# Two row-number tables instead of one, and a different placing of the first experts' reads, loads and splits, in an attention, ReLU-squared and routed-experts kernel

## The chip, the cores and the metric

The kernel runs on one core of one Trainium2 chip. The metric is device time in microseconds (us) of one execution, given as a median over runs.

## The reference

Three stages follow one another, all in float32 by value.

```python
# 1. attention, batch 4, 8 heads, 576 positions, 64 wide: a path downsampled by 4
#    (144 x 144, its result repeated 4 times) plus a local path, |i - j| < 4
x = (out_up + out_local)              # -> 2304 tokens x 512
# 2. a dense layer pair with squared ReLU (weights 512 x 2048 and 2048 x 512, stored as float64)
h = np.maximum(x @ w_in, 0.0)
x = (h * h) @ w_out
# 3. one expert of eight for each token
e_idx = np.argmax(x @ w_gate, axis=1)
gate_w = probs[np.arange(N), e_idx]   # softmax of x @ w_gate
eom = 1.0 / (1.0 + np.exp(-(x @ w_output_gate)))
for e in range(8):
    mask = e_idx == e
    ye = np.maximum(x[mask] @ w1[e], 0.0) @ w2[e]     # 512 -> 1024 -> 512
    out[mask] = gate_w[mask, None] * eom[mask, e, None] * ye
```

## The kernel before

**Dense stage.** The 2304 tokens are cut into nine chunks of 256 (`NCH = 9`), the 2048 hidden columns into 16 pieces of 128 (`NF = 16`, `FH = 8`). One step of the main loop does `l1(c, f)` (12 matmuls, line 473) for a piece f of a chunk c, and `l2` (6 matmuls, line 498) for the piece two steps back (`LAG = 2`). Every operand is held as two float32r parts, high and low, so a product is three matmuls. Between `l1` and `l2` of a piece stands a chain over three engines: ScalarE takes the ReLU out of PSUM (line 477), VectorE squares it and so frees the PSUM buffer (line 478), ScalarE rounds it to the high part (line 481), GpSimd subtracts to get the low part (line 482). There are two buffers of `ph` and of `g`, three of `gs`.

**Routing.** When a chunk's result is complete, `finish_y` copies it to SBUF and `routing` runs in three steps, interleaved with the next chunk's loop. It computes the gate scores, picks the expert of each token, computes the token's place in its expert's list, and then GpSimd writes the row numbers of the chunk's two tiles into a DRAM table `order` with two indirect DMAs of 128 four-byte elements each (line 586). A table `ytab` gets the rows themselves, from the SyncE queue (line 592). `order` has 8 lists of 2304 places; it is cleared at the start (line 168).

**First tiles.** In the last chunk (c = 8), at step f = 10, `first_rows` reads the first 128 places of the lists of experts 0 and 1 (tile `of`, line 657), casts them to integers on VectorE (line 659), gathers those rows (tile `xe`, line 662), and `first_part(0)` brings them through TensorE into PSUM (line 678). At the same step `experts[0].first()` and at f = 12 `experts[1].first()` load and split the four pieces of each expert's first weight matrix: a load is 512 KB on the SyncE queue into one of three buffers (tag `stg`, line 625), a split is a ScalarE copy of the piece (line 638) and a VectorE subtraction (line 639) of 128x1024 elements, after which the buffer is free again. At f = 14 the loads of the second matrix of expert 0 are written (line 628).

**After the last chunk.** The last chunk's routing adds its rows to the first tiles by matmuls with a one-hot matrix (line 712), writes its row numbers, and runs `first_layer(0)` (line 688). Then the whole table is read into `og` (line 838), transposed by TensorE (line 842), cast to `gi`, and used for all further gathers (line 878). By an issue-after edge `first_layer(1)` stands behind that transpose on TensorE. The second MoE stage then goes through the experts with branches on the number of tiles that each has.

The order of the instructions on each engine is chosen at build time by the scheduler of the framework, which may put an instruction ahead of the place where it is written. Each engine then takes its own instructions strictly in that order.

Of the kernel before, what the change touches and what calls it, by code (L numbers as in the profile page):

```python
# [10 lines left out]
F32 = mybir.dt.float32  # L11
F32R = mybir.dt.float32r
BF16 = mybir.dt.bfloat16
I32 = mybir.dt.int32
U32 = mybir.dt.uint32
AF = mybir.ActivationFunctionType
ALU = mybir.AluOpType
AX = mybir.AxisListType
#: Read as float32, the top half of a float64 times this has float32's exponent, three bits too low.
# [6 lines left out]
def attn_moe_kernel(  # L26
# [14 lines left out]
    nc = tc.nc  # L41
# [52 lines left out]
    order = dp.tile([E * NT, 1], F32, name="order")  # L94
# [16 lines left out]
    class Carved:  # L111
        """Buffers within larger tiles (each with the place that is free in it), by tag."""
# [55 lines left out]
    nc.gpsimd.dma_start(out=order.rearrange("(p c) o -> p (c o)", p=P), in_=none)  # L168
# [5 lines left out]
    def attention(b, hp, ap, psa):  # L174
# [51 lines left out]
        # local scores  # L226
# [86 lines left out]
        # downsampled P V  # L313
# [16 lines left out]
        # local P V  # L330
# [20 lines left out]
    def chain(units):  # L351
        """Units on one set of buffers: each starts in the middle of the one before it."""
        gens = [attention(*u) for u in units]

        def go(i, n):
            for _ in range(n if i < len(gens) else 0):
                next(gens[i], None)
                yield

        yield from go(0, 4)  # L360
        for i in range(len(gens)):
            yield from go(i, 3)
            yield from go(i + 1, 3)
            yield from go(i, 2)
            yield from go(i + 1, 1)
            yield from go(i, 1)
            if len(gens) == 1:
                yield from gens[i]
            else:
                go_on = gens[i]  # L370
                next(go_on, None)
                yield

# [14 lines left out]
    def f64_split(raw, hi, lo):  # L388
        """hi + lo of 512 columns of float64 words: float32's 24 bits, in two float32r parts."""
# [19 lines left out]
    def convert():  # L409
        """Both matrices of the first MoE in turn, a piece of 512 columns at a time."""  # L410
# [36 lines left out]
    def split_x(c, part):  # L447
        """The part of a chunk of x that is of its first (0) or another (1) of x's batches."""
        if c not in xc:
            xc[c] = mp.tile([P, 2, KC, CH], F32R, tag="xc", name=f"xc{c}")  # L450
        t, done = xc[c], 0
        while done < CH:
            b, s = divmod(c * CH + done, S)
            ln = min(CH - done, S - s)
            if part == (done > 0):
                for hp in range(HP):
                    src = carry[:, hp, :] if (c, part) == (2, 0) else xT[b, hp][:, s:s + ln]
                    hi = t[:, 0, hp, done:done + ln]
                    nc.scalar.activation(out=hi, in_=src, func=AF.Copy)
                    nc.vector.tensor_sub(out=t[:, 1, hp, done:done + ln], in0=src,  # L460
                                         in1=hi.bitcast(F32))
            done += ln
# [54 lines left out]
    def routing(c):  # L517
        """Puts the rows of y and their gates in ytab, their numbers in their experts' lists."""
# [66 lines left out]
        for i in range(2):  # L585
            nc.gpsimd.indirect_dma_start(  # L586
                out=order[:], out_offset=bass.IndirectOffsetOnAxis(ap=di[:, i:i + 1], axis=0),
# [21 lines left out]
    class Weights:  # L609
        """An expert's weights: four pieces for each layer are loaded, then put in two parts."""  # L610
# [30 lines left out]
        def first(self):  # L641
            self.place(0)
            for i in range(4):
                self.load(i)
                self.split(i)

# [6 lines left out]
    def first_rows():  # L653
        """What the first tiles of experts 0 and 1 hold before the last rows of y come."""
        of = const.tile([P, 2], F32, name="of")
        for i in range(2):
            nc.gpsimd.dma_start(out=of[:, i:i + 1], in_=order[NT * i:NT * i + P, :])
        oi = const.tile([P, 2], I32, name="oif")
        nc.vector.tensor_copy(oi, of)
# [11 lines left out]
        firsts.update(xe=xe, iota=iota2, xs=xs, hr=hrs)  # L671
        firsts["px"] = [first_part(0)]

# [19 lines left out]
    def last_rows(yr, dest, after):  # L693
        """The first tiles of experts 0 and 1, to which the last rows of y are added."""
# [89 lines left out]
    LAG, SX = 2, 4  # L784
    for s in range(len(seq) + LAG):
# [12 lines left out]
        if s < len(seq):  # L798
# [13 lines left out]
            if c == NCH - 1 and f == NF // 2 + 2:  # L812
                assert not routes
                first_rows()
                experts[0].first()
            if c == NCH - 1 and f == NF // 2 + 4:
                experts[1].first()
            if c == NCH - 1 and f == NF - 2:
# [14 lines left out]
    for i in range(3):  # L833
        experts[2].load(i, stages[i])

# [1 line left out]
    og = cv.tile([P, DM], I32, tag="tmp", name="og", bufs=TMPB).bitcast(F32)[:E * NTL // 2, 0:2 * P]  # L837
    nc.gpsimd.dma_start(out=og.rearrange("t (h p) -> t h p", h=2),
                        in_=order.rearrange("(t h p) o -> t h (p o)", h=2, p=P))
# [45 lines left out]
    def split_rows(xg, xs, g, name):  # L885
        """A tile's rows, transposed and in two parts; its gates and numbers to g."""
# [13 lines left out]
    def layer2(w2v, name):  # L900
        """The second layer of the tile that hs and gp belong to."""
# [14 lines left out]
    def hand_over(g, name, hr=hr):  # L916
        """The tile of hr and g becomes that of hs and gp."""
# [117 lines left out]
```

## Time and profile before

| | |
|---|---|
| median of 3 runs | 936.34 us |
| lowest and highest run | 930.26 and 936.98 us |
| profiled execution | span 932.8 us (the page gives no other time for it) |
| TensorE busy over the span | 854.6 us, 92% |
| VectorE, ScalarE, GpSimd busy | 426.7, 412.3, 361.5 us |
| DMA | 90.77 MB, mean 97 GB/s |

The profiled execution lies inside the spread of the runs, 3.5 us below their median. The rows further down come from it. Times in them are microseconds from the start of its span. PE is TensorE's matmuls, PEld its weight loads, DVE is VectorE, ACT is ScalarE, POOL is GpSimd, SP is SyncE; a q behind a name is the engine's own sequencer, where DMAs are issued. An arrow in brackets gives the idle time of the engine just before the row and what ended it.

### The profile page before, as it was taken

The page shows a single profiled execution, that of the slowest core. Times are in us where ns is not written, and L with a number is a line of the kernel's source. Part 1 is how long each engine was busy: PE and PEld are TensorE (multiplying, and loading weights), DVE is VectorE, ACT ScalarE, POOL GpSimd, SP SyncE. Part 2 cuts the span into 40 slices and gives each one's busy share as a digit, 9 for nine tenths or more (in the row PEclk, how much of TensorE's full clock was granted, in tenths as well). Part 3 has the DMA queues.
Part 4 walks back from the last instruction along what each step waited for, and adds up shares of the span by engine and source line. Part 5 has one row for each costly group of instructions (what it writes and reads, how often), then busy time and mean ns, then how long its engine had stood idle before and what let it go on. Part 6 is the DMA issues. An engine that isn't in the chain of part 4 may idle for free. (4 is left out here: it accounts for less than half of the span.)

```text
span 932.8 us, 16539 instructions
## 1 busy us (share of the span) xinstructions
PE 854.6 (92%) x6287; PEld 735.6 (79%) x6287; DVE 426.7 (46%) x910; ACT 412.3 (44%) x875; POOL 361.5 (39%) x450
## 2 busy tenths in 40 slices
PE   6568888999999999999999999778999899999995
PEld 5457677889989889889999899666777678878783
DVE  6999988533544433333222213332536564233110
ACT  6656556534454444443333324352536464243221
POOL 4876777542544533443222232342223322121111
PEclk9578988999999999999999999969999999999998
DMA  9963554111232212213000001754745944131111
GB/s 230 220 166 90 139 165 138 46 41 37 64 66 53 66 31 58 40 45 114 2 24 1 24 1 48 159 114 117 268 140 205 346 141 170 46 126 36 48 34 34
DMA packets 97602, 90.77 MB, mean 97 GB/s; under 512 B 64481, under 2 KB 77295, under 8 KB 97488
## 3 DMA queue, kind: packets, MB, share of 16 engines
q1 hardware_dynamic: 92096, 74.57, 27.9%
q0 software_dynamic: 5392, 14.74, 5.2%
q8 instruction: 65, 1.06, 0.5%
q14 instruction: 49, 0.40, 0.1%
HBM read 79.69 MB, written 10.38 MB: 97 GB/s over the span
## 5 line engine op out<-in xcount | busy, mean ns | idle before, releaser
L473 PE MATMUL ph<-xc,win 128*128 128x256 f32 x1728 | 254.1, 293 | 15.8 <-DVE g L478 8.1
L473 PEld LDWEIGHTS ph<-xc,win 128*128 128x128 f32 x1728 | 234.6, 195 | 30.4 <-DVE g L478 8.7
L498 PE MATMUL y<-wout,gs 128*128 128x512 f32 x864 | 232.0, 401 | 4.9 <-POOL gs L482 2.9
L482 POOL TENSOR_TENSOR gs<-g,gs 128x256 fp32r<-128x256 f32 x144 | 110.0, 767 | 189.2 <-ACT gs L481 107.4
L498 PEld LDWEIGHTS y<-wout,gs 128*128 128x128 f32 x864 | 152.7, 190 | 32.7 <-POOL gs L482 4.9
L478 DVE SCALAR_TENSOR_TENSOR g<-ph,g 128x256 f32<-128x256 f32 x144 | 60.2, 420 | 174.6 <-ACT g L477 173.8
L688 PE MATMUL ph<-we,xs 128*128 128x512 f32 x456 | 113.1, 403 | 8.3 <-ACTq L989 4.6
L905 PE MATMUL py<-we,hs 128*128 128x512 f32 x480 | 118.0, 401 | 2.1 <-DVEq L988 2.1
L477 ACT ACTIVATE g<-ph 128x256 f32<-128x256 f32 x144 | 55.2, 386 | 132.5 <-PE ph L473 119.5
L688 PEld LDWEIGHTS ph<-we,xs 128*128 128x128 f32 x456 | 84.6, 190 | 30.5 <-ACTq L989 5.8
L905 PEld LDWEIGHTS py<-we,hs 128*128 128x128 f32 x480 | 90.2, 190 | 23.3 <-issue 2.3
L878 POOL DMA_INDIRECT xg<-ytab,apt x35 | 40.9, 1169 | 112.4 <-ACT apt L691 50.1
L481 ACT ACTIVATE gs<-g 128x256 fp32r<-128x256 f32 x144 | 59.6, 417 | 56.0 <-DVE g L478 54.8
L912 POOL DMA_INDIRECT out_dram<-ob,oi x20 | 20.7, 1033 | 95.2 <-issue 39.1
L909 ACT ACTIVATE ob<-py,g 128x512 f32<-128x512 f32 x20 | 13.7, 687 | 97.1 <-PE py L905 97.1
L918 DVE COPY g<-g 128x2 f32<-128x2 f32 x21 | 3.5, 169 | 107.5 <-ACT ob L909 104.5
L691 ACT ACTIVATE apt<-ph 128x512 f32<-128x512 f32 x38 | 22.7, 598 | 50.1 <-PE ph L688 50.1
L639 DVE TENSOR_TENSOR we<-apt,we 128x1024 fp32r<-128x1024 f32 x31 | 37.0, 1238 | 10.8 <-ACT we L638 10.8
L894 DVE TENSOR_TENSOR xs<-px,xs 128x512 fp32r<-128x512 f32 x27 | 18.6, 689 | 44.8 <-ACT xs L891 44.5
L638 ACT ACTIVATE we<-apt 128x1024 fp32r<-128x1024 f32 x34 | 33.8, 1049 | 11.2 <-DMA apt<-in_moe_w_dram 8.7
L639 DVE TENSOR_TENSOR we<-stg,we 128x1024 fp32r<-128x1024 f32 x30 | 35.1, 1219 | 0.0
L586 POOL DMA_INDIRECT order<-row,di x18 | 18.6, 1033 | 42.4 <-DMA order<-row,di 18.1
(254 smaller groups left out, 1170.1 us busy)
## 6 DMA issues: line engine op xcount, KB each, us to landing
apt<-in_moe_w_dram SPq DMA_DIRECT2D x34, 512.0 KB
stg<-in_moe_w_dram SPq DMA_DIRECT2D x30, 512.0 KB
apt<-in_v_dram SPq DMA_DIRECT2D x52, 144.0 KB
raw<-in_moe_w_out_dram SPq DMA_DIRECT2D x11, 512.0 KB
raw<-in_moe_w_in_dram SPq DMA_DIRECT2D x11, 512.0 KB
ytab<-yr SPq DMA_DIRECT2D x18, 260.0 KB
apt<-in_q_dram SPq DMA_DIRECT2D x26, 144.0 KB
apt<-in_k_dram SPq DMA_DIRECT2D x26, 144.0 KB
```

Source lines behind the costliest of these rows:

```text
L473: nc.tensor.matmul(ph, lhsT=wv[:, wh, kk, :], rhs=x[:, xh, kk, :], start=(n == 0), stop=(n == 3 * KC - 1))
L477: nc.scalar.activation(out=g, in_=ph, func=AF.Relu)
L478: nc.vector.scalar_tensor_tensor(out=g, in0=ph, scalar=0.0, in1=g, op0=ALU.max, op1=ALU.mult)
L481: firsts["act"] = nc.scalar.activation(out=gs[:, 0, :], in_=g, func=AF.Copy).ins
L482: nc.gpsimd.tensor_sub(out=gs[:, 1, :], in0=g, in1=gs[:, 0, :].bitcast(F32))
L498: nc.tensor.matmul(yps[c][i], lhsT=gs[:, gh, P * i:P * i + P], rhs=woutv[f // FH][:, wh, f % FH, :], start=(f == 0 and n == 0), stop=(f == ...
L638: nc.scalar.activation(out=hi, in_=sv, func=AF.Copy)
L639: (nc.gpsimd if pool else nc.vector).tensor_sub(out=lo, in0=sv, in1=hi.bitcast(F32))
L688: nc.tensor.matmul(ph[h], lhsT=xs[:, a, P * kk:P * kk + P], rhs=w1v[:, b, kk, 512 * h:512 * h + 512], start=(n == 0), stop=(n == 3 * KC - 1))
L691: nc.scalar.activation(out=hr[:, 512 * h:512 * h + 512], in_=ph[h], func=AF.Relu)
L878: nc.gpsimd.indirect_dma_start(out=xg[:], out_offset=None, in_=ytab[:], in_offset=bass.IndirectOffsetOnAxis(ap=idx, axis=0))
L905: nc.tensor.matmul(py, lhsT=hs[:, a, P * kf:P * kf + P], rhs=w2v[:, b, kf, :], start=(kf == 0 and n == 0), stop=(kf == KF - 1 and n == 2))
```

## The change

There are two tables instead of one. The numbers of a chunk's first tile go to the first table, those of its second tile to the second; each place is written in one of them and stays zero in the other. What is read from both is added on VectorE: for `of` (now 128x2 four-byte elements from each table) and for `og`, whose second part is read from the SyncE queue. Both tables are cleared at the start. `first_rows` becomes a generator in three parts, at f = 9 (the reads of the tables), f = 11 (the addition, the gather) and f = 14 (`first_part(0)`). The loads and splits of the first matrices of experts 0 and 1 are written one by one at steps 8 to 14 of the last chunk, in a table `early` of (expert, piece, 0 for load or 1 for split). The loads of the second matrix of expert 0 are written at f = 15. The other lines of the diff only drop comments.

```diff
-    order = dp.tile([E * NT, 1], F32, name="order")
+    orders = [dp.tile([E * NT, 1], F32, name=f"order{i}") for i in range(2)]
...
-    nc.gpsimd.dma_start(out=order.rearrange("(p c) o -> p (c o)", p=P), in_=none)
+    for o in orders:
+        nc.gpsimd.dma_start(out=o.rearrange("(p c) o -> p (c o)", p=P), in_=none)
...
         for i in range(2):
             nc.gpsimd.indirect_dma_start(
-                out=order[:], out_offset=bass.IndirectOffsetOnAxis(ap=di[:, i:i + 1], axis=0),
+                out=orders[i][:], out_offset=bass.IndirectOffsetOnAxis(ap=di[:, i:i + 1], axis=0),
                 in_=row[:, 2 * c + i:2 * c + i + 1], in_offset=None)
...
-        def first(self):
-            self.place(0)
-            for i in range(4):
-                self.load(i)
-                self.split(i)
-
...
     def first_rows():
-        of = const.tile([P, 2], F32, name="of")
-        for i in range(2):
-            nc.gpsimd.dma_start(out=of[:, i:i + 1], in_=order[NT * i:NT * i + P, :])
+        of = const.tile([P, 2, 2], F32, name="of")
+        for t in range(2):
+            nc.gpsimd.dma_start(
+                out=of[:, t, :],
+                in_=orders[t].rearrange("(e n) o -> n (e o)", n=NT)[0:P, 0:2])
+        yield
         oi = const.tile([P, 2], I32, name="oif")
-        nc.vector.tensor_copy(oi, of)
+        nc.vector.tensor_tensor(out=oi, in0=of[:, 0, :], in1=of[:, 1, :], op=ALU.add)
...
+        yield
         firsts["px"] = [first_part(0)]
+        yield
...
+    early = {FH: [(0, 0, 0), (0, 1, 0), (0, 2, 0)],
+             FH + 2: [(0, 0, 1), (0, 3, 0), (0, 1, 1), (1, 0, 0)],
+             FH + 3: [(0, 2, 1), (1, 1, 0)],
+             FH + 4: [(0, 3, 1), (1, 2, 0)],
+             FH + 5: [(1, 0, 1), (1, 3, 0), (1, 1, 1)],
+             FH + 6: [(1, 2, 1), (1, 3, 1)]}
...
-            if c == NCH - 1 and f == NF // 2 + 2:
-                assert not routes
-                first_rows()
-                experts[0].first()
-            if c == NCH - 1 and f == NF // 2 + 4:
-                experts[1].first()
-            if c == NCH - 1 and f == NF - 2:
+            if c == NCH - 1:
+                if f == FH + 1:
+                    assert not routes
+                    rows = first_rows()
+                if f in (FH + 1, FH + 3, NF - 2):
+                    next(rows)
+                for e, i, of in early.get(f, ()):
+                    if of and i == 0:
+                        experts[e].place(0)
+                    (experts[e].split if of else experts[e].load)(i)
+            if c == NCH - 1 and f == NF - 1:
                 for i in range(4, 7):
                     experts[0].load(i)
                 experts[0].load(7, firsts["hr"][1])
...
     og = cv.tile([P, DM], I32, tag="tmp", name="og", bufs=TMPB).bitcast(F32)[:E * NTL // 2, 0:2 * P]
-    nc.gpsimd.dma_start(out=og.rearrange("t (h p) -> t h p", h=2),
-                        in_=order.rearrange("(t h p) o -> t h (p o)", h=2, p=P))
+    og2 = cv.tile([P, DM], I32, tag="tmp", name="og2", bufs=TMPB).bitcast(F32)[:E * NTL // 2, 0:2 * P]
+    for o, eng, src in ((og, nc.gpsimd, orders[0]), (og2, nc.sync, orders[1])):
+        eng.dma_start(out=o.rearrange("t (h p) -> t h p", h=2),
+                      in_=src.rearrange("(t h p) o -> t h (p o)", h=2, p=P))
+    nc.vector.tensor_add(out=og, in0=og, in1=og2)
```

## Rows read from the trace of the kernel before

**Rows 1.** Windows of the span: busy us of each engine, then granted clock, DMA share, GB/s
```profile
400.00:500.00 100.00, 100.00 (x706) 90.25 (x705) 28.09 (x97) 35.75 (x101) 31.95 (x48) 1.00 0.13 42
...
580.00:600.00 20.00, 16.19 (x100) 13.92 (x99) 11.29 (x18) 9.64 (x18) 7.20 (x9) 1.00 0.80 159
600.00:620.00 20.00, 14.77 (x73) 12.10 (x72) 2.04 (x5) 6.21 (x11) 9.62 (x8) 0.83 0.33 107
620.00:640.00 20.00, 16.26 (x91) 14.49 (x90) 10.81 (x33) 8.04 (x15) 4.51 (x3) 0.74 0.66 155
```

**Rows 2.** Timeline of PE in the last chunk: start, us, instruction, idle before it
```profile
584.46 1.60 PE L473 MATMUL ph<-xc,win 128*128 128x256 f32 x12
...
587.29 1.59 PE L473 MATMUL ph<-xc,win 128*128 128x256 f32 x12
...
592.12 0.73 PE L498 MATMUL y<-wout,gs 128*128 128x512 f32 x2 [1.01 <-POOL gs L482]
...
597.18 1.69 PE L473 MATMUL ph<-xc,win 128*128 128x256 f32 x12 [2.81 <-DVE g L478]
...
604.39 0.86 PE L473 MATMUL ph<-xc,win 128*128 128x256 f32 x5 [1.72 <-DVE g L478]
...
607.37 0.79 PE L498 MATMUL y<-wout,gs 128*128 128x512 f32 x1 [1.89 <-POOL gs L482]
607.97 1.97 PE L678 MATMUL pxf<-ident,apt 128*128 128x128 f32 x8
...
615.08 1.65 PE L498 MATMUL y<-wout,gs 128*128 128x512 f32 x6
```

**Rows 3.** Timelines of POOL: the clearing, table writes and reads, the gather
```profile
2.76 0.77 POOL L168 DMA_DIRECT2D order<-init  x1
...
12.89 1.26 POOL L261 TENSOR_TENSOR apt<-apt 128x640 f32<-128x640 f32 x1 [6.36 <-DVE apt L260]
...
590.32 0.99 POOL L586 DMA_INDIRECT order<-row,di  x1 [3.99 <-DMA order<-row,di]
...
597.56 1.18 POOL L657 DMA_DIRECT2D of<-order  x2 [4.80 <-DMA order<-row,di]
...
604.28 1.02 POOL L662 DMA_INDIRECT apt<-ytab,oif  x1 [4.77 <-DVE oif L659]
...
632.23 0.96 POOL L586 DMA_INDIRECT order<-row,di  x1 [4.83 <-DMA order<-row,di]
640.34 0.60 POOL L838 DMA_DIRECT2D og<-order  x1 [7.15 <-DMA order<-row,di]
```

**Rows 4.** Timelines of ACT and DVE: splits and the cast
```profile
577.65 2.94 ACT L638 ACTIVATE we<-apt 128x1024 fp32r<-128x1024 f32 x3
...
594.48 1.06 ACT L638 ACTIVATE we<-apt 128x1024 fp32r<-128x1024 f32 x1 [5.59 <-DMA apt<-in_moe_w_dram]
...
603.84 0.17 DVE L659 CAST oif<-of 128x2 int32<-128x2 f32 x1 [5.24 <-DMA of<-order]
```

**Rows 5.** Timeline of PE behind the last chunk
```profile
630.31 1.06 PE L678 MATMUL pxf<-ident,apt 128*128 128x128 f32 x8
...
638.48 1.18 PE L688 MATMUL phf<-we,xsf 128*128 128x512 f32 x4
...
643.24 0.34 PE L842 MATMUL po<-ident,og 72*128 72x72 f32 x2 [3.58 <-DMA og<-order]
...
643.45 4.59 PE L688 MATMUL phf<-we,xsf 128*128 128x512 f32 x12
...
648.66 3.05 PE L688 MATMUL phf<-we,xsf 128*128 128x512 f32 x12
```

**Rows 6.** Windows of 1 us: granted clock, DMA share, GB/s are the last three
```profile
588.00:589.00 1.00, 1.00 0.00 0
...
602.00:603.00 1.00, 1.00 0.98 357
...
637.00:638.00 1.00, 1.00 (x7) 0.82 (x5) 0.00 (x0) 0.29 (x1) 0.00 (x0) 1.00 0.75 296
```

## The prediction

> **What bounds the kernel now.** I read the windows of the span first. In the steady loop TensorE is busy for all of 100 us at full clock, though GpSimd waits for table writes there too; nothing that shortens those waits can gain anything in that stretch. In 580 to 640 TensorE is busy for 47.2 of 60 us (16.19, 14.77, 16.26) and the granted clock sinks to 0.83 and 0.74 [rows 1]. That is where the change works, so the second view is TensorE's timeline there. A step of the loop lasts 2.83 us (587.29 - 584.46). Then come four idle times: 1.01 us on GpSimd's subtraction, 2.81 on VectorE's square, 1.72 on a square again, 1.89 on a subtraction, 7.43 us together; behind the last one TensorE runs at its lower level for a while (8 matmuls of the first part take 1.97 us, later 1.06) [rows 2, 5]. The reader should see that each named releaser only passes a delay on. The other engines' timelines say what that engine was held by. The 1.01 stands behind GpSimd's second table write, which waited 3.99 us for the first one to land. The 2.81 stands behind a ScalarE split that waited 5.59 us for its load. The 1.72 stands behind the cast of `of`, which held VectorE for 5.24 us. The 1.89 stands behind the gather, for which GpSimd waited 4.77 us [rows 3, 4]. Behind the chunk the table chain is plain: the second write waits 4.83 us, the read of `og` 7.15 us, and TensorE stands idle for 3.58 us; the next 12 matmuls take 4.59 us, where 12 of the same take 3.05 shortly after [rows 3, 5].
>
> **Part 1: two tables.** The second write of a chunk no longer waits for the first. In the steady loop this is worth nothing [rows 1]. In the last chunk it removes the 3.99 us wait, and behind it the 4.83.
>
> Behind the loop, step by step. GpSimd was free again at 632.23 - 4.83 = 627.40, so the second write can be issued by 627.40 + 0.96 = 628.4 [rows 3]. When does it land? At best one issue later than the first did, 632.23 + 0.96 = 633.2; at worst 7.15 us behind its issue, as before, 635.5 [rows 3]. The read of `og` takes 0.60 us to issue and lands 2.30 us later as before (643.24 - 640.94), or 5.10 as `of` did while loads were moving (603.84 - 598.74) [rows 3 to 5]. That gives 636.1 to 641.2. The second half, `og2`, goes through SyncE's queue behind three loads whose bytes move until 638 [rows 6]; it lands at 638 to 640.3. The addition is one small VectorE operation; the cast of the same size class takes 0.17 [rows 4]. So TensorE can transpose between 638.2 and 641.4, and it is free at 638.48 + 1.18 = 639.66 [rows 5]. The idle time left is 0 to 1.75 us. I take 0.9, nearer to the row with loads in flight, as they are here. Of 3.58 that leaves a gain of 2.7. An idle time of 2.81 did not bring the clock down (the 12 matmuls behind it took 1.69 against 1.60) [rows 2], so the 4.59 - 3.05 = 1.54 us come back as well. **Tail: 4.2 us**, between 1.8 (idle 1.75, clock down anyway) and 5.1 (both in full). It carries to the end, since all later gathers hang on this transpose.
>
> The second clearing costs GpSimd some 0.77 us at 3.5; it later idles 6.36 us before 12.89 [rows 3], which hides it. Uncovered it would cost 0.8 at most.
>
> **Part 2: the first rows in three parts.** The reads go to f = 9, the addition and the gather to f = 11, the first part to f = 14. With both writes issued back to back, they should have landed at about 590.32 + 0.99 = 591.3 instead of 597.56, when the reads were issued before [rows 3]. The reads are twice as many small elements. I have no row for that; from below it costs nothing (two DMAs as before), from above as much again as the one landing seen, 5.10. The nearest is the pair of before, so I take some 1 us more than it. The values are then there between 594.8 (591.3 + 1.18 + 2.30) and 597.6 or 598.6, against 603.84 [rows 3, 4]. Who is queued behind the waits? Behind GpSimd's wait for the tables stand the subtractions, which `l2` needs; behind VectorE's addition the squares, which free PSUM for `l1`. Both waits now fall into the time in which TensorE waits for the late load anyway, until 597.18 [rows 2].
>
> **Part 3: loads and splits spread.** The work is the same: 8 loads, 8 ScalarE copies, 8 subtractions. The place at which they are written is only a priority. In the trace of before three splits that are written at f = 10 run at 577.65, seven microseconds ahead of the matmuls of that step at 584.46 [rows 2, 4]. So I expect ScalarE and VectorE to keep much the same order, and the wait of 5.59 us for a load to remain: I count **nothing** for this part. Were it to work in full, it would give the 2.81 and 1.01 back; that is a rival. Writing the loads of the second matrix one step later costs nothing: nothing needs that matrix before the second MoE stage, behind 648 [rows 5].
>
> **The sum for the loop.** With TensorE at 597.18 as before, three steps of 2.83 for f = 13 to 15 end at 605.67; the first part at full clock is 1.06; two `l2` without an `l1` beside them take 1.65 each (the price of the one at 615.08). That ends at 610.0. Before it ended at 615.08 + 1.65 = 616.73 [rows 2, 5]. So 6.7 us, if neither the addition nor the gather stalls TensorE again. If VectorE meets the addition ahead of the square that it does at 597, and the values come up to 1.5 us late, and GpSimd then issues two gathers of 1.02 us each ahead of its subtractions, 2.8 of that go back. I take half: 5.3. **Together 5.3 + 4.2 = 9.5 us.** The profiled execution would go from 932.8 to 923.3. It stands 3.5 us below the median of the runs; from that median, 936.3 - 9.5 = **926.8 us**.
>
> **A rule that speaks against this.** The reads of `of` had 5.10 us from issue to landing, `og` 2.30; the loads beside `of` were still moving 357 GB/s in 602 to 603, and `of` counts as landed at 603.84, just behind them [rows 4 to 6]. The Trainium skill, "DMA: Bandwidth & Descriptors", section "Queues, rings and completion order", says why this need not be chance: the completion signal of a transfer is a strongly ordered write, which lands only when every earlier write of that DMA engine, across its queues, has landed. The trace agrees. By that rule an earlier read of the tables falls in with other loads and its wait is carried along, which is the second rival.
>
> **The rivals.**
> First, everything works: the load stall goes too. From 587.29 five steps of 2.83 end at 601.44, with 1.06 and 3.30 at 605.8; 10.9 us in the loop and 5.1 behind it give 16.0, so **920.3**. For it: the loads are written earlier than the splits by one to three steps. Against: a load waits for the buffer of a split, whatever the place in the text.
> Second, the removed waits are taken over: the reads of the tables now wait on GpSimd for both writes, with subtractions behind, and land behind loads. The loop gains 1.5 of its 6.7, the tail 2.7 without the clock: 4.2, so **932.1**. For it: four waits in a row were passed on in this way before [rows 3, 4].
> Third, slower: after a table write the DMA engines stand still (0 GB/s in 588 to 589, while loads had been issued) [rows 6]; the split waiting at that time got its data only at 594.48. If two writes and the wider reads, sent closely together, each hold the loads up once more by those 5.59 us, the late split comes 11.2 us later, the square behind it too, and the loop loses 11.2 where it gains nothing; with 1.8 left from the tail that is 9.4 slower, **945.7**. It decides from the point at which the load of expert 1's third piece is behind both. Against: the same small elements were sent before as well, only one after another.
> That the spreading does nothing at all is already what I assume in the sum.
>
> **How the numbers follow.** Forecast 0.46, all works 0.21, taken over 0.27, slower 0.06. A measurement of this kernel tells about 1%, here 9.4 us, from no change: the line lies at 927.0 and 945.7. The forecast stands almost on it; a little more than half of its share and all of the first rival lie below, 0.47. Above 945.7 lies 0.06 at most, and 0.47 lies between. The range goes from 917, the first rival with the clock kept up behind the chunk as well, to 936, the second with the lower bounds of both terms.
>
> **What would show it.** In the profile after: no wait of the second table write for a table; `og` issued before 637 of the old scale, and TensorE idle less than 1.8 us before the transposes, with full clock behind them; the cast (now an addition) waiting under 2 us; no idle time of TensorE above 1 us between the late split and the end of the chunk. If ScalarE no longer waits for a load of an expert, part 3 works and I am too high. If the table reads hold GpSimd for 4 us or more, with TensorE waiting on its subtraction, the second rival is right. I would be wrong altogether if TensorE stood idle longer before 600 than now.

## The result and the profile after

The changed kernel takes 943.56 us (median of 9 runs, 939.5 to 947.14) against 935.91 (9 runs, 930.26 to 937.96): a ratio of 1.0081, 95% interval 1.0061 to 1.0102. It is slower by 0.8%, where 926.8 was forecast and the range ended at 936. The profiled execution has a span of 943.4 us, 10.6 more than the one of before.

The windows of the span, of the changed kernel, which answer to [rows 1]:

```profile
400.00:500.00 100.00, 100.00 (x784) 90.00 (x783) 30.01 (x100) 36.04 (x100) 32.71 (x49) 1.00 0.14 43
580.00:600.00 20.00, 19.03 (x125) 16.38 (x124) 11.38 (x32) 9.73 (x20) 8.45 (x12) 1.00 0.52 113
600.00:620.00 20.00, 16.05 (x93) 13.43 (x94) 6.07 (x10) 7.99 (x15) 10.70 (x11) 1.00 0.63 153
```

The stretch of 400 to 500 is as full as before. From 580 to 620, where the changed loop code works, TensorE is busier than before and keeps its clock. So the time was lost elsewhere, and the waits name two places. From the view of waits (engine, line waited for: us in total, times, longest):

```profile
PE pgf L733 <- DVE g L738: 5.4, 1, 5.4
PE ktp L191 <- DMA apt<-in_k_dram: 5.3, 1, 5.3
```

**Where the spans differ.** I cut each trace at the same instructions: ScalarE's copy of the finished result of a chunk (`yr<-y`, line 510 in the changed kernel) for chunks 3, 4, 7 and 8, and the start of the last row of `po` transposes in the timeline (line 857). Chunks are counted from 0, so 8 is the last. One trace of before is not enough here: it has a longer last chunk and a shorter second MoE stage than the other kernels with one table. So the first group holds three kernels with serial writes, whose times are alike (two of them are experiments below, 0.9991 and 1.0024 of before), and the second the two traces of the changed kernel. Each row is one execution, and those of late_clear, two_from_7 and add_behind further down are the fastest of their kernel, 3.6, 2.5 and 1.4 us below its median, while that of after_again is the slowest, 1.9 us above; one of the ten runs of sum_on_pe took 1646 us and is left out of its ratio.

| kernel | end of chunk 3 | chunk 4 | chunks 5 to 7 | chunk 8 | chunk 8 to `po` | `po` to end | span |
|---|---|---|---|---|---|---|---|
| before | 343.7 | 67.0 | 147.7 | 58.1 | 26.7 | 289.6 | 932.8 |
| spread_only | 344.4 | 66.3 | 147.7 | 56.3 | 24.7 | 292.6 | 931.9 |
| clear_only | 345.5 | 66.4 | 147.7 | 55.9 | 25.2 | 292.0 | 932.7 |
| after | 346.3 | 73.1 | 147.7 | 53.7 | 30.1 | 292.6 | 943.4 |
| after_again | 345.8 | 72.7 | 147.7 | 51.9 | 29.0 | 292.6 | 939.6 |

Means of the two groups: 1.5 us later at the end of chunk 3, 6.3 us more in chunk 4, nothing in chunks 5 to 7, 4.0 less in chunk 8, 4.0 more from there to `po`, 1.2 more behind it. That makes 9.0 of the 9.0 us by which the mean spans differ (941.5 against 932.5).

**Chunk 4.** The timeline of the changed kernel there (GpSimd, SyncE, TensorE):

```profile
380.76 1.08 POOL L588 DMA_INDIRECT order<-row,di  x1 [0.15 <-issue]
382.14 0.97 POOL L588 DMA_INDIRECT order<-row,di  x1 [0.30 <-issue]
...
383.01 1.25 SPq L182 DMA_DIRECT2D apt<-in_k_dram  x2
...
394.33 1.19 PE L191 MATMUL ktp<-ident,apt 96*128 96x96 f32 x6 [5.33 <-DMA apt<-in_k_dram]
```

and the same rows of the kernel before:

```profile
378.23 1.07 POOL L586 DMA_INDIRECT order<-row,di  x1 [0.15 <-issue]
...
384.36 0.99 POOL L586 DMA_INDIRECT order<-row,di  x1 [3.61 <-PE qtp L189]
...
380.48 1.25 SPq L180 DMA_DIRECT2D apt<-in_k_dram  x2
...
387.96 0.69 PE L189 MATMUL ktp<-ident,apt 96*128 96x96 f32 x6 [1.38 <-DMA apt<-in_k_dram]
```

Both writes now leave GpSimd just ahead of the load of the attention's k. TensorE gets to the transposes of k 7.5 us after the issue of the load before (387.96 - 380.48) and 11.3 us after it now. Windows of 2 us of the changed kernel (columns as above):

```profile
386.00:388.00 2.00, 2.00 (x17) 1.83 (x17) 0.00 (x0) 1.24 (x2) 1.44 (x2) 1.00 0.34 75
388.00:390.00 2.00, 1.00 (x6) 0.67 (x4) 1.08 (x2) 0.65 (x3) 0.00 (x0) 1.00 0.31 70
390.00:392.00 2.00, 0.00 (x0) 0.00 (x0) 0.00 (x0) 0.00 (x0) 0.00 (x0) 1.00 0.30 61
392.00:394.00 2.00, 0.00 (x0) 0.00 (x0) 0.00 (x0) 0.00 (x0) 0.00 (x0) 0.55 0.56 131
394.00:396.00 2.00, 1.67 (x9) 1.70 (x10) 0.00 (x0) 0.44 (x1) 0.64 (x1) 0.50 0.13 38
```

The reader should see two windows in which no engine does anything while the DMA engines move only 61 to 131 GB/s, and the granted clock sinking to its lower level (0.50, 1.2 GHz) with TensorE's idle time. Before, the DMA engines moved 177 GB/s (DMA share 0.79) in 384 to 386, just before TensorE took k. Of the 6.1 us that chunk 4 lost between the two profiles, 3.95 are the longer wait (5.33 - 1.38); the rest was lost behind it, where the granted clock was 0.50 until 398 and 0.74 from 398 to 400 (before, it stayed at 1.00): the six transposes take 1.19 us instead of 0.69.

**The last chunk.** The changed kernel's timeline, what answers to [rows 2 to 4]:

```profile
586.32 2.95 ACT L640 ACTIVATE we<-apt 128x1024 fp32r<-128x1024 f32 x3
...
592.97 1.06 ACT L640 ACTIVATE we<-apt 128x1024 fp32r<-128x1024 f32 x1 [3.12 <-DMA apt<-in_moe_w_dram]
...
594.32 1.81 POOL L588 DMA_INDIRECT order<-row,di  x1 [0.30 <-issue]
...
604.93 0.76 POOL L653 DMA_DIRECT2D of<-order  x1 [3.37 <-DMA order<-row,di]
...
610.26 0.16 DVE L658 TENSOR_TENSOR oif<-of 128x2 int32<-128x2 f32 x1 [2.72 <-DMA of<-order]
...
601.61 0.73 PE L500 MATMUL y<-wout,gs 128*128 128x512 f32 x2 [1.99 <-POOL gs L484]
...
606.50 0.74 PE L500 MATMUL y<-wout,gs 128*128 128x512 f32 x2 [1.31 <-POOL gs L484]
...
620.76 0.60 ACT L510 ACTIVATE yr<-y 128x512 f32<-128x512 f32 x1 [0.94 <-PE y L500]
```

The second write no longer waits for the first (0.30 us, issue only). But its read was held up until 604.93, 8.8 us after the issue had ended at 596.13. Counted from the end of chunk 7 (558.38 before, 567.05 now) the values of the first rows are there only 2.3 us earlier (43.2 against 45.5 us). The longest idle times of TensorE are 1.99 and 1.31 us, the largest five are 4.9 us together against 7.43 in four before, and the clock stays at 1.00. On ScalarE and VectorE the sixth of the eight splits now stands a step earlier among the loop's instructions than before, and on VectorE the addition stands one square earlier than the cast did; ScalarE's waits for the loads are 9.1 us together against 8.7, with a shorter longest one.

**Behind the last chunk.** The changed kernel's timeline, what answers to [rows 3, 5]:

```profile
630.54 1.10 POOL L588 DMA_INDIRECT order<-row,di  x1 [2.50 <-DVE hit L699]
631.95 1.94 POOL L588 DMA_INDIRECT order<-row,di  x1 [0.30 <-issue]
...
631.94 1.47 SPq L627 DMA_DIRECT2D apt<-in_moe_w_dram  x2
643.49 0.33 SPq L852 DMA_DIRECT2D og<-order  x1
...
647.13 0.42 DVE L854 TENSOR_TENSOR og<-og,og 72x256 f32<-72x256 f32 x1 [11.04 <-DMA og<-order]
647.47 0.15 DVE L738 COPY g<-pgf 128x2 f32<-128x2 f32 x1
647.54 0.68 DVE L716 TENSOR_TENSOR xsf<-pxf,xsf 128x512 fp32r<-128x512 f32 x1
...
647.68 0.59 PE L733 MATMUL pgf<-apt,ident 128*128 128x2 f32 x2 [5.37 <-DVE g L738]
...
650.83 0.44 PE L857 MATMUL po<-ident,og 72*128 72x72 f32 x2
...
651.14 4.82 PE L689 MATMUL phf<-we,xsf 128*128 128x512 f32 x12
```

SyncE could read the second table only at 643.49, 9.6 us after the write's issue had ended (633.89). The addition waited 11.04 us on VectorE, and two operations that have nothing to do with the tables stood behind it: the copy of a gate, and the subtraction that makes the low part of the first rows of expert 1. TensorE waited for the copy in the middle of expert 0's first layer and stood idle for 5.37 us; expert 1's first layer needs the subtraction. The 12 matmuls behind `po` took 4.82 us, with a granted clock of 0.50 up to 654; before, they took 4.59.

### The profile page after: what moved, and what is told of

Read it like the earlier page. It is cut to its first block, busy times and chain, and to the rows that moved or that the text cites. A ratio compares the mean times of both kernels' runs of the same rounds, so it can differ in the third digit from the quotient of the medians.

```text
span 943.4 us, 16551 instructions
## 1 busy us (share of the span) xinstructions
PE 856.5 (91%) x6287; PEld 735.2 (78%) x6287; DVE 430.2 (46%) x911; ACT 413.7 (44%) x875; POOL 366.6 (39%) x451
## 5 line engine op out<-in xcount | busy, mean ns | idle before, releaser
L484 POOL TENSOR_TENSOR gs<-g,gs 128x256 fp32r<-128x256 f32 x144 | 112.9, 785 | 210.5 <-ACT gs L483 134.0
L893 POOL DMA_INDIRECT xg<-ytab,apt x35 | 41.6, 1188 | 127.5 <-ACT apt L692 52.7
L692 ACT ACTIVATE apt<-ph 128x512 f32<-128x512 f32 x38 | 22.8, 599 | 52.9 <-PE ph L689 52.9
L205 DVE TENSOR_REDUCE apt<-apt 128x144 f32<-128x576 f32 x26 | 19.5, 750 | 40.6 <-ACT apt L197 40.6
```

Source lines behind the costliest of these rows:

```text
L484: nc.gpsimd.tensor_sub(out=gs[:, 1, :], in0=g, in1=gs[:, 0, :].bitcast(F32))
L692: nc.scalar.activation(out=hr[:, 512 * h:512 * h + 512], in_=ph[h], func=AF.Relu)
L893: nc.gpsimd.indirect_dma_start(out=xg[:], out_offset=None, in_=ytab[:], in_offset=bass.IndirectOffsetOnAxis(ap=idx, axis=0))
```

## The experiments

Ratios are to the kernel before on the same chip. The first four runs shared one chip (932.0 us before), the next four another (932.68), the last four a third (932.59). The stage lengths are those of the table above.

| run | median us | ratio (95%) | end of chunk 3 | chunk 4 | chunk 8 | 8 to `po` |
|---|---|---|---|---|---|---|
| spread_only | 932.06 | 0.9991 (0.9968 to 1.0015) | 344.4 | 66.3 | 56.3 | 24.7 |
| clear_only | 934.11 | 1.0024 (1.0003 to 1.0044) | 345.5 | 66.4 | 55.9 | 25.2 |
| late_clear | 935.33 | 1.0036 (1.0013 to 1.0059) | 342.5 | 67.6 | 52.7 | 28.8 |
| sum_on_pe | 936.96 | 1.0046 (1.0021 to 1.0071) | 346.5 | 71.9 | 52.3 | 24.5 |
| after_again | 939.51 | 1.0091 (1.0064 to 1.0118) | 345.8 | 72.7 | 51.9 | 29.0 |
| two_from_7 | 934.25 | 1.0026 (1.0007 to 1.0046) | 344.6 | 65.8 | 51.3 | 29.2 |
| loads_behind | 935.41 | 1.0050 (1.0026 to 1.0074) | 346.7 | 71.0 | 52.7 | 23.1 |
| best | 935.59 | 1.0046 (1.0026 to 1.0066) | 345.7 | 66.4 | 54.0 | 30.9 |
| add_behind | 935.54 | 1.0036 (1.0019 to 1.0054) | 345.2 | 71.4 | 51.2 | 25.7 |
| best2 | 930.4 | 0.9973 (0.9958 to 0.9988) | 343.0 | 65.8 | 52.9 | 25.4 |
| best3 | 927.22 | 0.9952 (0.9930 to 0.9974) | 344.5 | 66.0 | 54.6 | 23.0 |
| best_early2 | 931.04 | 0.9984 (0.9965 to 1.0002) | 348.0 | 65.8 | 51.6 | 25.3 |

### Parts of the change alone

**spread_only**: the new placing of reads, loads and splits, with one table read and copied as before.

```diff
-    orders = [dp.tile([E * NT, 1], F32, name=f"order{i}") for i in range(2)]
+    order = dp.tile([E * NT, 1], F32, name="order")
...
-        nc.vector.tensor_tensor(out=oi, in0=of[:, 0, :], in1=of[:, 1, :], op=ALU.add)
+        nc.vector.tensor_copy(oi, of)
...
```

> One table as before, with the new placing of the first rows' reads, the loads and the splits. Theory (the placing changes nothing, since the order of the instructions on ScalarE, VectorE and GpSimd comes out as before; the loss comes from the second table): the time of before, within 0.3%. Rival (later splits and loads cost the time): 3 to 8 us slower than before.

Measured: 0.9991. In its trace ScalarE, VectorE and GpSimd have their instructions in the order of before, by operation and tile; on TensorE the first part stands one matmul later. The spreading alone does nothing that this run could show. It does not tell what the spreading does together with the second table, where a split and the addition stand a step earlier; no run has two tables with the old placing.

**clear_only**: the kernel before with a second table that is only cleared.

```diff
+    other = dp.tile([E * NT, 1], F32, name="other")
...
-    nc.gpsimd.dma_start(out=order.rearrange("(p c) o -> p (c o)", p=P), in_=none)
+    for o in (order, other):
+        nc.gpsimd.dma_start(out=o.rearrange("(p c) o -> p (c o)", p=P), in_=none)
```

> The kernel before, with a second table that is cleared at the start and never used. Theory (the second clearing holds GpSimd 0.8 us at the start, the scheduler then puts the attention's instructions in another order, and chunks 1 to 3 end 2.5 us later, as in the changed kernel): 1 to 3 us slower than before, chunk 3 ending 2 to 3 us later; no stall of 5 us at a load of k. Rival (that shift is chance of one execution): no difference. Second rival (the reordering makes the whole loss ahead of the last chunk, the stall at k too): 8 us slower.

Measured: 1.0024, with an interval that only just leaves out 1. The order of the attention's instructions is another one from the start on. VectorE of this kernel:

```profile
7.50 0.75 DVE L205 TENSOR_REDUCE apt<-apt 128x144 f32<-128x576 f32 x1 [7.50 <-ACT apt L197]
8.17 0.98 DVE L159 COPY mask<-init 64x320 f32<-64x320 f32 x2
```

and of the kernel before:

```profile
4.48 0.99 DVE L158 COPY mask<-init 64x320 f32<-64x320 f32 x2 [4.48 <-POOL init L153]
7.28 0.75 DVE L203 TENSOR_REDUCE apt<-apt 128x144 f32<-128x576 f32 x1 [1.81 <-ACT apt L195]
```

An operation that GpSimd does in its idle time made the scheduler change what VectorE does first. Chunk 3 ends at 345.5 instead of 343.7. TensorE does not wait for k in this trace.

**late_clear**: the changed kernel, but the second table is cleared later, by a copy of the first on SyncE's queue.

```diff
-    for o in orders:
-        nc.gpsimd.dma_start(out=o.rearrange("(p c) o -> p (c o)", p=P), in_=none)
+    nc.gpsimd.dma_start(out=orders[0].rearrange("(p c) o -> p (c o)", p=P), in_=none)
...
+    nc.sync.dma_start(out=orders[1].rearrange("(p c) o -> p (c o)", p=P),
+                      in_=orders[0].rearrange("(p c) o -> p (c o)", p=P))
```

> The changed kernel, but the second table is cleared by a copy of the first one from SyncE's queue, so that GpSimd has one clearing at the start as before; the attention's instructions then stand in the order of before. Theory: the first 2.5 us of the loss go, the stall at the load of k (two table writes sent back to back ahead of it) and the loss behind the last chunk stay: 3 to 7 us slower than before. Rival (the reordering makes all that is lost ahead of the last chunk): the last chunk starts as early as before and the kernel is level with it or faster.

Measured: 1.0036, 3.4 us slower than before as expected, and some 0.5% better than the changed kernel (1.0081 and 1.0091). Chunk 3 ends early (342.5). TensorE waits 1.99 us for k in this trace and not 5.33, though the two writes stand equally close ahead of the load (376.97, 378.35, load at 379.21):

```profile
379.21 1.25 SPq L181 DMA_DIRECT2D apt<-in_k_dram  x2
...
387.19 0.69 PE L190 MATMUL ktp<-ident,apt 96*128 96x96 f32 x6 [1.99 <-DMA apt<-in_k_dram]
```

It gets k 8.0 us after the issue, and chunk 4 takes 67.6. So this part of the theory, that the stall stays, failed in this execution: two writes do not always cost the same, and the last chunk starts here as early as before, as the rival said. What else must be in flight for the 11.3 us is open. The trace is of a run of 931.75 us, where the median is 935.33, so it does not say what the stall is in the others. The tail is as long as in the changed kernel.

### The load of k

**after_again** is the changed kernel once more, beside the next three on their chip; no edit.

> The changed kernel as it is, beside the others on the same chip: 6 to 10 us slower than before; the stall of 4 to 6 us at a load of k in chunk 4 again, and TensorE waiting 5 us ahead of the transposes of the list.

It gave 1.0091 and the same stages (chunk 4 72.7, wait for k 4.5 us); TensorE's wait in the middle of the first layer is 3.4 us, less than the 5 expected.

**two_from_7**: two tables only for chunks 7 and 8; until then both writes of a chunk go to the first table, one after the other as before.

```diff
-                out=orders[i][:], out_offset=bass.IndirectOffsetOnAxis(ap=di[:, i:i + 1], axis=0),
+                out=orders[i if c >= NCH - 2 else 0][:], out_offset=bass.IndirectOffsetOnAxis(ap=di[:, i:i + 1], axis=0),
```

> The changed kernel, but chunks 0 to 6 write both of their tiles' numbers to the first table, so that the second write waits for the first there, as before; the last two chunks use two tables. Theory (two table writes sent back to back ahead of a load of k hold that load up for twice as long): the stall of TensorE at the transpose of k in chunk 4 falls from 4 to 6 us to under 1.5 us, and the kernel is 3 to 6 us faster than the changed one. Rival (the stall comes from the other order of the attention's instructions): it stays, and the time with it.

Measured: 1.0026 against 1.0091 on the same chip, 0.65% or some 6 us. From its timeline:

```profile
379.13 1.07 POOL L588 DMA_INDIRECT order<-row,di  x1 [0.16 <-issue]
...
384.88 0.99 POOL L588 DMA_INDIRECT order<-row,di  x1 [3.23 <-DMA order<-row,di]
...
381.37 1.25 SPq L182 DMA_DIRECT2D apt<-in_k_dram  x2
...
387.68 0.69 PE L191 MATMUL ktp<-ident,apt 96*128 96x96 f32 x6 [0.20 <-DMA apt<-in_k_dram]
```

With one write ahead of the load and the other behind it, k is there 6.3 us after its issue and chunk 4 is back to 65.8. The five traces with early clearing and two tables throughout have 71.0 to 73.1; the four further ones whose chunks up to 6 use one table (best, best2, best3, best_early2) have 65.8 to 66.4, with late or early clearing. This shows that the 6 us of chunk 4 hang on the parallel writes, and that the wait between the two writes which the change removed had been useful there: it kept the second write behind the issue of the load. Over all traces TensorE took k 8.8 to 11.3 us after the issue with two writes ahead and early clearing, 8.0 us in late_clear, and 6.2 to 7.5 us with one write ahead. So the parallel writes are needed for the loss, but late_clear shows that they do not bring it in full by themselves.

### The tail

**sum_on_pe**: no addition on VectorE. TensorE sums the tables in PSUM, by matmuls with the identity, and GpSimd issues both reads.

```diff
-    for o, eng, src in ((og, nc.gpsimd, orders[0]), (og2, nc.sync, orders[1])):
+    for o, eng, src in ((og, nc.gpsimd, orders[0]), (og2, nc.gpsimd, orders[1])):
...
-    nc.vector.tensor_add(out=og, in0=og, in1=og2)
...
-        tr = nc.tensor.transpose(out=po[:, h * E * NTL // 2:(h + 1) * E * NTL // 2],
...
+        for i, o in enumerate((og, og2)):
+            tr = nc.tensor.matmul(po[:, h * E * NTL // 2:(h + 1) * E * NTL // 2],
+                                  lhsT=o[:, P * h:P * h + P],
+                                  rhs=ident[:E * NTL // 2, :E * NTL // 2],
+                                  start=(i == 0), stop=(i == 1))
```

> The changed kernel, but both parts of the list are read from GpSimd's queue and summed by TensorE in PSUM (four small matmuls instead of two transposes), with no addition on VectorE. Theory (the read on SyncE's queue, which waits 10 us for the second table and holds a load of expert 2 behind it, and the addition that holds VectorE's split of the first rows for 11 us, cost what is lost behind the last chunk): 5 to 7 us faster than the changed kernel, TensorE idle ahead of the transposes 0 to 3.6 us instead of 5.4. Rival (the second table just lands late, whoever reads it): the wait moves to TensorE, and 0 to 2 us are gained.

Measured: 1.0046, 3 to 4 us better than the changed kernel (1.0081 and 1.0091, on other chips), less than expected. Its timeline (GpSimd, TensorE):

```profile
629.52 1.94 POOL L588 DMA_INDIRECT order<-row,di  x1 [0.30 <-issue]
...
640.21 0.55 POOL L852 DMA_DIRECT2D og<-order  x1 [6.21 <-DMA order<-row,di]
...
642.83 0.89 PE L857 MATMUL po<-ident,og 72*128 72x72 f32 x6 [0.50 <-DMA og<-order]
643.52 3.05 PE L689 MATMUL phf<-we,xsf 128*128 128x512 f32 x12
```

TensorE waits 0.50 us ahead of the transposes and no longer in the middle of the first layer (5.37 there in the changed kernel), and the 12 matmuls behind run at full clock (3.05). The second table's read was still held until 640.21, 8.75 us after the issue of its write had ended.

**loads_behind**: sum_on_pe with the second read on SyncE again and the three loads for expert 2 behind it on that queue.

```diff
-    for i in range(3):
-        experts[2].load(i, stages[i])
...
+    with tc.issue_after(rd.ins):
+        for i in range(3):
+            experts[2].load(i, stages[i])
```

> The kernel in which TensorE sums the two parts of the list, but the second part is read from SyncE's queue and the three loads of expert 2 are put behind that read. Theory (the second table's write is held up by those loads): it lands 4 to 6 us after its issue instead of 8.7, the list is read 3 us sooner, and TensorE does not wait ahead of the transposes; what the loads lose is 4 to 8 us of lead and may come back as a wait in the second MoE stage, so the time itself is open, from 3 us faster to 3 us slower than that kernel. Rival (the pair of writes needs that time by itself): it lands 8 to 9 us after its issue as in that kernel, and nothing is gained.

Its timeline (GpSimd, SyncE):

```profile
629.22 1.93 POOL L588 DMA_INDIRECT order<-row,di  x1 [0.30 <-issue]
...
635.77 0.33 SPq L850 DMA_DIRECT2D og<-order  x1
636.20 1.36 SPq L627 DMA_DIRECT2D apt<-in_moe_w_dram  x3
```

Without the loads beside it the second write was readable 4.6 us after its issue had ended (635.77 - 631.15) instead of 8.75. In the other kernels with two tables, all with loads issued beside the write, it took 8.4 to 10.1 us; in best3 below, without them, 4.7. That shows that two or three loads of 512 KB hold up the write, at a price of some 4 us here. The rule quoted in the prediction from the Trainium skill ("DMA: Bandwidth & Descriptors", "Queues, rings and completion order") would do this if the loads' writes count as earlier ones; the run does not tell it from the loads' taking their share of the DMA engines. The transposes ran without a wait, 23.1 us after the chunk instead of 24.5. In the time of the kernel none of this showed (1.0050, against 1.0046 on another chip).

**add_behind**: the changed kernel with one edge, so that VectorE takes the addition only behind the subtraction for expert 1's first rows.

```diff
-    nc.vector.tensor_add(out=og, in0=og, in1=og2)
+    with tc.issue_after(firsts["lo"]):
+        nc.vector.tensor_add(out=og, in0=og, in1=og2)
```

> The changed kernel with one instruction moved: VectorE's addition of the two parts of the list stands behind its split of expert 1's first rows. The reads stay where they are. Theory (in its queue the addition holds that split and the copy of a gate, for which TensorE waits in the middle of a first layer): TensorE ends that layer 3 to 5 us sooner, then waits for the list; the transposes come where they came, within 1 us, so that the time gained is 0 to 2 us. Rival (the addition in the queue is what is lost behind the last chunk): 3 to 4 us faster than the changed kernel.

Measured: 1.0036, about 0.5% or 4.5 us better than the changed kernel (on other chips). My theory there was too low and the rival right. Chunk 8 to `po` is 25.7, as in the kernels with one table, so the addition's place on VectorE is what made the tail longer. TensorE of this kernel:

```profile
641.25 0.48 PE L858 MATMUL po<-ident,og 72*128 72x72 f32 x2 [1.76 <-DVE og L855]
...
641.60 4.45 PE L689 MATMUL phf<-we,xsf 128*128 128x512 f32 x12
```

The idle time is at the upper end of what I had forecast (0 to 1.75 us), and the clock was lost all the same (4.45 us, not 3.05).

### A version without the costs

**best**: late_clear, two_from_7 and sum_on_pe together (the copy that clears the second table and the sum on TensorE are the lines shown above).

```diff
-    for o in orders:
-        nc.gpsimd.dma_start(out=o.rearrange("(p c) o -> p (c o)", p=P), in_=none)
+    nc.gpsimd.dma_start(out=orders[0].rearrange("(p c) o -> p (c o)", p=P), in_=none)
...
-                out=orders[i][:], out_offset=bass.IndirectOffsetOnAxis(ap=di[:, i:i + 1], axis=0),
+                out=orders[i if c >= NCH - 2 else 0][:], out_offset=bass.IndirectOffsetOnAxis(ap=di[:, i:i + 1], axis=0),
```

> Three mends together: the late clearing from SyncE, two tables for the last two chunks alone, the sum on TensorE. Theory (the three places make up the loss, and the last chunk gains 4 us): 3 to 6 us faster than before. Rival (the last chunk's gain is given back by the second table's late landing and by the second stage): within 0.3% of before.

Measured: 1.0046; the theory failed, and it is more than the rival's 0.3%, too. From its timeline of TensorE:

```profile
636.72 0.70 PE L858 MATMUL po<-ident,og 72*128 72x72 f32 x2 [4.93 <-DMA og<-order]
```

The scheduler had put the sum of the first table's part into the first layer, behind its first four matmuls, where TensorE waited 4.93 us for the first table: the same fault as the addition's, on another engine.

**best2**: best with the transposes behind the last matmul of the first tile's first layer.

```diff
...
+    with tc.issue_after(firsts["mm"].ins):
+        for h in range(2):
+            for i, o in enumerate((og, og2)):
...
```

> The three mends together (late clearing, two tables for the last two chunks, sum on TensorE), and the matmuls that sum the list stand behind the whole first layer of expert 0, not in its middle, where TensorE waited 4.9 us for the first table. Theory (that wait was what the three mends lacked): 3 to 6 us faster than they were, 0 to 4 us faster than before. Rival (the second part lands late, whatever TensorE does): as the three mends, 3 to 4 us slower than before.

Measured: 0.9973, some 2 us faster than before, as the theory said; 8 to `po` fell from 30.9 to 25.4.

**best3**: best2 with the loads of expert 2 behind the second read, as in loads_behind.

```diff
-    for i in range(3):
-        experts[2].load(i, stages[i])
...
+    with tc.issue_after(rd.ins):
+        for i in range(3):
+            experts[2].load(i, stages[i])
```

> As the last one, and the three loads of expert 2 stand behind the read of the second part of the list. Theory: the list is there 3 us sooner, but the first branch of the second MoE stage, which TensorE reached sooner and waited at for 4.4 us when only the loads were moved, gives most of it back: within 2 us of the last kernel. Rival (the earlier list counts in full): 3 us faster than that.

Measured: 0.9952, the fastest. Beside best2 on the same chip it is 2 to 3 us ahead, with overlapping intervals, so between the theory and the rival. From its timeline (SyncE, TensorE):

```profile
630.55 0.33 SPq L851 DMA_DIRECT2D og<-order  x1
...
635.67 1.01 PE L860 MATMUL po<-ident,og 72*128 72x72 f32 x8
636.48 3.04 PE L688 MATMUL phf<-we,xsf 128*128 128x512 f32 x12
```

The second write's issue ended at 625.83; it was readable 4.7 us later (630.55 - 625.83). No wait stands ahead of the transposes and the clock is full behind them. 8 to `po` is 23.0 us against 24.7 to 26.7 in the kernels with one table: 2.6 below their mean, of the 4.2 that the change was to bring in the tail.

**best_early2**: best2 with the second table cleared at the start on GpSimd, as in the change.

```diff
-    nc.gpsimd.dma_start(out=orders[0].rearrange("(p c) o -> p (c o)", p=P), in_=none)
+    for o in orders:
+        nc.gpsimd.dma_start(out=o.rearrange("(p c) o -> p (c o)", p=P), in_=none)
```

> As the kernel with the three mends and the matmuls of the list behind the first layer, but with both tables cleared at the start on GpSimd. Theory (the second clearing there costs 2 us by the other order of the attention's instructions): 1 to 3 us slower than with the late clearing. Rival (both orders are worth the same): within 1 us.

Measured: 0.9984 against 0.9973. Chunk 3 ends 5 us later in the trace (348.0 against 343.0), but the intervals overlap, so this run doesn't settle the clearing's cost.

## Why the prediction was wrong, point by point

**"In the steady loop this is worth nothing [rows 1]": the first step that failed.** The row showed 100 us of a dense loop of which I took the whole. That stretch is as full after as before. But chunk 4 is not steady: beside its steps runs attention whose load of k SyncE issues just behind the table writes, and there the trace of before already had a wait of 1.38 us that I hadn't looked for. I asked what the waits cost and not what they held back. Removing them cost 6.3 us there: two_from_7, which puts them back in these chunks alone, has chunk 4 at 65.8. What else made it 6.3 us and not the 1 us of late_clear's trace stays open. The signs that I had named all look at the last chunk and behind it, so none could show this. The mechanism is the one of my third rival, two writes sent closely together that hold a load up, but at another load: in the last chunk, where I had placed it, the longest wait of a split for its load went from 5.59 us to 3.12. I had priced it at 5.59 for each write; what was measured is 3.95 for both and some 2 for the lower clock behind. That its 945.7 lies near the measured time is chance.

**"Tail: 4.2 us": the second step that failed, in sign.** It was minus 4.0. Two of its parts were wrong. The second write was to be readable "at worst 7.15 us behind its issue"; it took 9.6 with loads of 512 KB issued beside it (8.4 to 10.1 in the other kernels, 4.6 without them in loads_behind). From the start of the first write to the second table's read passed 14.05 us before (640.34 - 626.29, [rows 3]) and 12.95 after (643.49 - 630.54): of the gain by issuing the second write early 1.1 us were left. And "the addition is one small VectorE operation" priced the operation and not its wait: I didn't say what stands behind it on VectorE. Behind the 11.04 us stood what TensorE needed next. With the addition moved (add_behind) the idle time was 1.76, my upper bound; with the sum on TensorE 0.50; with both causes removed none. The clock did not come back at 1.76 us idle (4.45), but did at 0.50 (3.05).

**The clearing, "which hides it"**: GpSimd's time is indeed hidden. But the operation changed the order in which the scheduler put the attention's instructions. The eight kernels with early clearing end chunk 3 at 346.1 on average (344.6 to 348.0), the six without at 344.0 (342.5 to 345.7). In time it is 0.24% in clear_only (0.03 to 0.44), 0.1% in the pair best2 and best_early2, which is not resolved: a small loss, weakly shown.

**The loop, 5.3 us.** It gained 4.0 against the three kernels with serial writes, 4.4 against the trace of before alone. The sign and the size were right, the size in part by luck, since the landing behind it was wrong: both writes were to be readable a microsecond after the second's issue, and the first rows 5 to 9 us earlier. The second table was readable 8.8 us after its issue, and the rows came 2.3 us earlier. The 2.8 us that the forecast lets go back do not follow from their terms either (1.5 and two gathers of 1.02 make 3.5, half of which would leave 4.9). Some of the second rival is in this: GpSimd's second read waited 3.37 us, and TensorE 1.99 and 1.31 for GpSimd. The gain needs the second table, since spread_only (56.3) and clear_only (55.9) have none of it, but whether it also needs the new placing was not tested.

**Part 3, nothing**: right for the part alone (spread_only, 0.9991). The three splits that I took as evidence run 19.27 us after the end of chunk 7 in both kernels (577.65 - 558.38 and 586.32 - 567.05). But the wait of 5.59 us did not remain in the changed kernel, where the sixth split stands a step earlier; which of the parts did that is open.

**The sum** would have been -9.5; it was 1.5 + 6.3 - 4.0 + 4.0 + 1.2 = 9.0 in the spans. The 1.2 us behind `po` come from the one trace of before: against spread_only and clear_only it is 0.3.

## What to carry to other kernels

A wait that costs nothing where it stands may be what keeps a transfer out of the way of another: before removing it in a loop, look up in every stage what is issued shortly behind it, not only the stage in which it is seen to hurt. An operation that waits for data is priced by what its engine has queued behind it, so put an edge on it when the scheduler chooses the order. And where a small write is on the path, hold the large loads back until it can be read.

## What the runs showed of the hardware that was not expected

- A write of 128 four-byte elements to DRAM was readable 4.6 and 4.7 us after its issue had ended with no load issued meanwhile (loads_behind, best3), and 8.4 to 10.1 us with loads of 512 KB issued beside it (nine traces; 8.75 in sum_on_pe, 9.6 in after).
- The second of two such writes, issued 0.30 us behind the first, took 1.81 and 1.94 us to issue in the last chunk and behind it, against 0.99 and 0.96 where it waited for the first [rows 3]; in chunk 4 it took 0.97. The loads beside it are not the reason: without them it took 1.93 and 1.94 (loads_behind, best3). The reason is open.
- The load of k (two DMAs of 144 KB) came 6.3, 7.5, 8.0 and 11.3 us after its issue (two_from_7, before, late_clear, after). In the last case the DMA engines moved 61 to 75 GB/s for the 6 us from 386 to 392. Why two writes ahead cost 8.0 in one and 11.3 in the other stays open.
